# Two staging buffers instead of three for q and k, and w_in loaded by column halves, in a fused attention and gMLP kernel

## The chip, the cores and the metric

The kernel runs on one core of a Trainium2 chip. The core has a matrix engine (TensorE, PE in the profile; its weight loads are PEld), a vector engine (VectorE, DVE), a scalar engine (ScalarE, ACT), GpSimd (POOL) and a queue engine (SyncE, SP). Each runs its own instruction stream in order; they meet at semaphores. Data between main memory and the on-chip memory is moved by 16 DMA engines; here SP issues DMAs on one queue (q1 in the profile) and POOL on another (q0). The metric is the device time of one execution in microseconds.

## The reference

Two blocks follow one another. The first is attention with a window and sinks: 4 batches, 8 heads, 768 positions, head size 64; position s sees positions s-127 to s and the first 4. The second is a gated MLP over the positions.

```python
scores = 0.125 * q @ k^T ; keep = is_sink | in_window       # per batch and head
a = softmax(where(keep, scores, -1e9)) ; x = a @ v           # x: (4, 768, 512)
h = gelu_tanh(x @ w_in)                                      # w_in: (512, 1024)
u, v = h[..., :512], h[..., 512:]
v_n = (v - mean) / sqrt(var + 1e-6) * g_ln
v_s = einsum('ts,bsd->btd', w_sg, v_n) + b_sg                # w_sg: (768, 768)
out = x + (u * v_s) @ w_out                                  # w_out: (512, 512)
```

The columns of w_in are thus of two kinds: the first 512 give u, the last 512 give the v of the MLP.

## The kernel before

**Pairs.** Attention goes by pairs of heads: 16 pairs, numbered n from 0, four to a batch. For each pair the kernel loads k and q (`load_qk`, line 79, on SP's queue, 384 KB each as float32 into the pool `loads`) and v (`load_v`, line 86, on POOL's queue, cast to bf16 on the way, 128 bytes per row and head; four tiles `v_bufs` in turn). Line 179 (`repack`) casts k and q to bf16 and joins the two heads: pair 0 on VectorE, all others on POOL. Once the cast has read a staging tile, that tile is free for a later load; the pool gives tiles out in turn, so its number of buffers says how many pairs back the cast lies that a load must wait for. Line 185 transposes k and q on TensorE (`keys`, `queries`), line 192 copies the result to SBUF on ScalarE, line 202 copies the four sink columns into `sk` on POOL.

**One pass of the loop** over n does the scores of pair n (line 220), their exponentials (224) and the mask (231), the sinks' scores (235, 237), and the product with v of pair n-1 (`values`, lines 265, 268, 271). In each group of three query tiles, line 271 adds the sinks' part from `vsink`, one tile with the sink rows of v for all pairs, loaded by two small DMAs on POOL's queue (line 132) right behind the first v tile. At the start of pass n POOL casts pair n+2, issues the v load of pair n+2 and then the weights that are due (`load_weights(n)`): w_in in passes 0 to 3, w_sg in pass 4, b_sg, g_ln and w_out in pass 5. `load_qk(n+3)` stands in pass n, but SP's queue holds nothing else before the first transpose by DMA (line 281), so at the start a load is issued as soon as its buffer is free.

**The MLP** of a batch follows when its four pairs are done: `hidden` computes the v half (`hidden_v`, line 293, w_in's last 512 columns) and then the u half (`hidden_u`, line 305, the first 512); `inverse_root` and `normalise` (333) work on VectorE. The spatial product (343) and the projection (354) are put into a list of fillers that are dealt out between the attention steps of the next batch. Results go out on SP's queue (360). After the first batch, three pairs in four have their columns transposed by DMA (281), also on SP's queue. The order of all instructions on each engine is the order of the program text; nothing reorders it.

A last part (`stable_path`) runs only if a sum is out of range; it doesn't run with these inputs.

Of the kernel before, what the change touches and what calls it, by code (L numbers as in the profile page):

```python
# [17 lines left out]
def kernel(  # L18
# [14 lines left out]
    nc = tc.nc  # L33
# [5 lines left out]
    d_ff = moe_w_in.shape[1]  # L39
    DF = d_ff // 2  # L40
    NT = S // 128
    HP = H // 2
    KD = DM // 128
# [4 lines left out]
    NH = S // 2  # L48

    consts = ctx.enter_context(tc.tile_pool(name="consts", bufs=1))  # L50
    loads = ctx.enter_context(tc.tile_pool(name="loads", bufs=3))
    work = ctx.enter_context(tc.tile_pool(name="work", bufs=2))
    small = ctx.enter_context(tc.tile_pool(name="small", bufs=4))
    ps_s = ctx.enter_context(tc.tile_pool(name="ps_s", bufs=2, space=PSUM))
# [88 lines left out]
    w_in_sb = consts.tile([128, KD, d_ff], BF16, name="w_in_sb")  # L143
# [4 lines left out]
    wsgT = consts.tile([128, NT, S], BF16, name="wsgT")  # L148

    def load_weights(n):  # L150
        if n < KD:
            nc.gpsimd.dma_start(out=w_in_sb[:, n, :],
                                in_=moe_w_in[128 * n:128 * (n + 1), :])
        elif n == 4:
            for c in (slice(0, HT), slice(HT, NT)):
                nc.gpsimd.dma_start(
                    out=wsg_sb[:, c, :],
                    in_=moe_w_sg.rearrange("(c p) s -> p c s", p=128)[:, c, :])
        elif n == 5:
            nc.gpsimd.dma_start(out=b_bc, in_=moe_b_sg.partition_broadcast(128))  # L160
            nc.gpsimd.dma_start(out=g_sb, in_=moe_g_ln.rearrange("(c p) -> p c", p=128))
            nc.gpsimd.dma_start(out=w_out_sb,
                                in_=moe_w_out.rearrange("(c p) f -> p c f", p=128))
# [351 lines left out]
    for n in range(NP):  # L515
        if n + 2 < NP:
            repack(n + 2, G)
            load_v(n + 2)
        load_weights(n)
        value = (lambda i: values(n - 1, i)) if n > 0 and valued < n - 1 else (lambda i: None)  # L520
        points = (HT + 1) * ((HP - n) % HP)
# [79 lines left out]
```

## Time and profile before

| | |
|---|---|
| median of 3 runs | 192.22 us (190.65 to 193.03) |
| the profiled execution | 192.91 us |
| its span, first to last instruction | 191.2 us |
| TensorE busy | 159.4 us, 83% |
| VectorE busy | 152.4 us, 80% |
| ScalarE busy | 115.9 us, 61% |
| GpSimd busy | 57.2 us, 30% |
| q1 (SP): q, k, transposes, results | 20.65 MB, 35.9% of the DMA engines' time |
| q0 (POOL): v, sinks, weights | 6.31 MB, 35.3% |

Busy time is the time in which an engine executes; waiting and issuing aren't in it. The DMA shares are means over the whole span; the first 48 us are far above them (nine tenths or more in the page's slices from 5 to 48 us). The megabytes count what is written, so v and the weights, which become bf16, have half of what is read.

### The profile page before, as it was taken

The numbers are of one execution on the slowest core, as the hardware profiler recorded it, in microseconds if no ns is written. First come the engines' busy times: TensorE is split into PE (matmuls) and PEld (weight loads), VectorE is DVE, ScalarE is ACT, GpSimd is POOL, SyncE is SP. The second block draws the span as 40 slices with busy tenths as digits, with TensorE's granted clock in tenths as the row PEclk, the third lists the DMA queues.
The fourth block names the chain that finished last, engine by engine and source line by source line (L and its number), as shares of the span: only waits on it lengthen the run. The fifth ranks groups of instructions, "written<-read, shape, count | busy, mean of one in ns | idle before, by whom it ended". The sixth has DMA issues, their size and how long they took to land.

```text
span 191.2 us, 3722 instructions
## 1 busy us (share of the span) xinstructions
PE 159.4 (83%) x1407; PEld 88.7 (46%) x1407; DVE 152.4 (80%) x362; ACT 115.9 (61%) x159; POOL 57.2 (30%) x98
## 2 busy tenths in 40 slices
PE   0661977879969999989979999899799979998960
PEld 0321655535553655545535555355355444545420
DVE  5780578879974999869889999698999976989960
ACT  2381699976871766866796686966966533740000
POOL 7497567970024016145006024163000000000000
PEclk9999999999975999999999999999999999999997
DMA  5999999999276075999653869996202172000072
GB/s 183 287 304 261 254 235 210 156 197 189 47 206 41 3 206 62 256 301 167 46 125 89 81 216 183 322 225 43 41 3 41 55 211 111 0 0 3 0 279 66
DMA packets 46777, 27.27 MB, mean 143 GB/s; under 512 B 33632, under 2 KB 43104, under 8 KB 46752
## 3 DMA queue, kind: packets, MB, share of 16 engines
q1 hardware_dynamic: 19360, 20.65, 35.9%
q0 software_dynamic: 27392, 6.31, 35.3%
q8 instruction: 13, 0.21, 0.5%
q14 instruction: 12, 0.10, 0.2%
HBM read 24.81 MB, written 6.29 MB: 163 GB/s over the span
## 4 chain that ended last, share of the span: by engine, by line
PE 44%; DVE 30%; ACT 11%; DMA 8%; issue 4%; POOL 0%; DVEq 0%
PE vs L343 11%; PE o_ps L354 10%; DMA vsink<-in_v_dram 8%; ACT ex L224 6%; DVE st L297 5%; PE sc L220 5%; DVE ex L231 4%; PE hv L293 4%; PE cps L185 4%; DVE vn L333 3%; DVE gv L346 3%; PE hu L305 3%; PE av L265 3%; DVE o_sb L357 2%; ACT kT L192 2%
## 5 line engine op out<-in xcount | busy, mean ns | idle before, releaser
L224 ACT ACTIVATE ex<-sc 128x1024 bf16<-128x1024 f32 (+1 forms) x48 | 45.6, 958 | 19.4 <-PE sc L220 19.1
L343 PE MATMUL vs<-wsgT,vn 128*128 128x384 bf16 x192 | 38.3, 339 | 2.6 <-DVE vn L333 1.0
L231 DVE TENSOR_TENSOR ex<-ex,mask 128x1024 bf16<-128x1024 bf16 x32 | 24.4, 764 | 3.1 <-ACT ex L224 3.1
L343 PEld LDWEIGHTS <-vn 128*128 128x128 bf16 x192 | 18.3, 101 | 16.9 <-issue 4.3
L354 PE MATMUL o_ps<-w_out_sb,gT 128*128 128x512 bf16 x96 | 24.1, 379 | 0.8 <-DVE o_sb L357 0.8
L293 PE MATMUL hv<-w_in_sb,xT 128*128 128x512 bf16 x96 | 22.8, 379 | 2.2 <-DVE xT L246 1.8
L305 PE MATMUL hu<-xT,w_in_sb 128*128 128x384 bf16 x128 | 23.6, 325 | 0.0
L179 POOL CAST k_bf<-k_sb 128x768 bf16<-128x768 f32 x15 | 12.8, 850 | 36.0 <-DMA k_sb<-in_k_dram 29.9
L265 PE MATMUL av<-v_sb,ex 128*128 128x65 bf16 x192 | 19.0, 198 | 5.1 <-DMA v_sb<-in_v_dram 3.2
L346 DVE SCALAR_TENSOR_TENSOR gv<-vs,g_sb,b_bc 128x384 bf16<-128x384 f32 x32 | 19.6, 612 | 3.0 <-PE vs L343 3.0
L295 ACT ACTIVATE v_all<-hv 128x512 f32<-128x512 f32 x24 | 14.3, 597 | 11.9 <-PE hv L293 11.8
L202 POOL COPY sk<-kT 64x4 bf16<-64x4 bf16 x32 | 7.0, 218 | 46.9 <-ACT kT L192 45.9
L265 PEld LDWEIGHTS <-ex 128*128 128x128 bf16 x192 | 14.9, 100 | 13.0 <-issue 5.7
L220 PE MATMUL sc<-qT,kT 64*128 64x256 bf16 x192 | 19.3, 285 | 1.2 <-DVE qT L194 1.1
L297 DVE BATCH_NORM_STATS2 st<-v_all 128x6 f32<-128x512 f32 x24 | 16.4, 683 | 4.8 <-ACT v_all L295 4.6
L308 ACT ACTIVATE uT<-hu 128x384 bf16<-128x384 f32 x32 | 15.7, 490 | 7.1 <-PE hu L305 6.9
L276 DVE TENSOR_TENSOR x<-av,inverses 128x384 bf16<-128x384 f32 x32 | 17.8, 557 | 1.1
L192 ACT COPY kT<-cps 128x768 bf16<-128x768 bf16 x16 | 12.7, 794 | 9.3 <-PE cps L185 9.3
L357 DVE TENSOR_TENSOR o_sb<-o_ps,x 128x512 f32<-128x512 f32 x24 | 16.5, 687 | 2.0 <-PE o_ps L354 1.7
L268 PE MATMUL av<-v_sb,ex 128*128 128x65 bf16 x160 | 17.4, 197 | 0.0
L86 POOL DMA_DIRECT2D v_sb<-in_v_dram x16 | 16.5, 1032 | 0.0
L305 PEld LDWEIGHTS <-w_in_sb 128*128 128x128 bf16 x128 | 12.1, 97 | 8.3 <-issue 1.2
(72 smaller groups left out, 232.5 us busy)
## 6 DMA issues: line engine op xcount, KB each, us to landing
k_sb<-in_k_dram SPq DMA_DIRECT2D x16, 384.0 KB, 6.0
q_sb<-in_q_dram SPq DMA_DIRECT2D x16, 384.0 KB, 6.5
out_dram<-o_sb SPq DMA_DIRECT2D x24, 256.0 KB, 3.7
v_sb<-in_v_dram POOLq DMA_DIRECT2D x16, 192.0 KB, 6.7
wsg_sb<-in_moe_w_sg_dram POOLq DMA_DIRECT2D x2, 576.0 KB, 9.6
w_in_sb<-in_moe_w_in_dram POOLq DMA_DIRECT2D x4, 256.0 KB, 11.7
w_out_sb<-in_moe_w_out_dram POOLq DMA_DIRECT2D x1, 512.0 KB, 10.3
b_bc<-in_moe_b_sg_dram POOLq DMA_DIRECT2D x1, 384.0 KB, 8.9
```

Source lines behind the costliest of these rows:

```text
L220: nc.tensor.matmul(sc[:, hl, w:w + n_q], kT[rows, 128 * j:128 * (j + 1)], qT[rows, 128 * j:128 * j + n_q], start=True, stop=True)
L224: nc.scalar.activation(out=part, in_=sc[:, :, 0:w], func=AF.Exp, scale=scale)
L231: nc.vector.tensor_mul(part, part, m)
L265: nc.tensor.matmul(av[:, m, hl, :], probs(i, hl, 0), v_sb[:, hl, i, :], start=(m == 0 and hl == 0), stop=False)
L276: nc.vector.tensor_mul(x_sb[b][:, hp, HT * c:HT * (c + 1), :].rearrange("p i (h d) -> p i h d", h=2), av[:, :, :, 0:64], rcp.to_broadcast( ...
L293: nc.tensor.matmul(h_ps, xT[b][:, c, 128 * j:128 * (j + 1)], w_in_sb[:, c, DF:], start=(c == 0), stop=(c == KD - 1))
L297: nc.vector.bn_stats(out=st, in_=v_alls[b][:, j, :])
L305: nc.tensor.matmul(h_ps[:, 0:NH], w_in_sb[:, c, 128 * f:128 * (f + 1)], xT[b][:, c, NH * n:NH * (n + 1)], start=(c == 0), stop=(c == KD - 1))
L343: nc.tensor.matmul(vs[:, 0:NH], vns[b][:, si, 128 * f:128 * (f + 1)], wsgT[:, si, cols], start=(si == 0), stop=(si == NT - 1))
L346: nc.vector.scalar_tensor_tensor(out=gv, in0=vs[:, 0:NH], scalar=g_sb[:, f:f + 1], in1=b_bc[:, cols], op0=ALU.mult, op1=ALU.add)
L354: nc.tensor.matmul(o_ps, gTs[b][:, c, 128 * t:128 * (t + 1)], w_out_sb[:, c, :], start=(c == 0), stop=(c == KU - 1))
L357: nc.vector.tensor_add(o_sb.rearrange("p (h d) -> p h d", h=HP), o_ps.rearrange("p (h d) -> p h d", h=HP), x_sb[b][:, :, t, :])
```

## The change

The pool `loads` gets two buffers per name instead of three, so k and q of pair n+2 wait for the cast of pair n (before: pair n+3 for pair n). w_in, which was loaded in four DMAs of one block of 128 rows and all 1024 columns, is loaded in four DMAs of two blocks of rows and 512 columns, the last 512 columns (the MLP's v half) in passes 0 and 1 and the first 512 (u) in passes 2 and 3. The bytes are the same.

```diff
-    loads = ctx.enter_context(tc.tile_pool(name="loads", bufs=3))
+    loads = ctx.enter_context(tc.tile_pool(name="loads", bufs=2))
...
     def load_weights(n):
-        if n < KD:
-            nc.gpsimd.dma_start(out=w_in_sb[:, n, :],
-                                in_=moe_w_in[128 * n:128 * (n + 1), :])
+        if n < 4:
+            half = slice(DF, d_ff) if n < 2 else slice(0, DF)
+            cs = slice(KD // 2 * (n % 2), KD // 2 * (n % 2 + 1))
+            nc.gpsimd.dma_start(
+                out=w_in_sb[:, cs, half],
+                in_=moe_w_in.rearrange("(c p) f -> p c f", p=128)[:, cs, half])
```

## The prediction

> **What bounds the kernel now.** I read the chain that ended last first, for where the time to the end is spent, then the engine timelines around the piece that stands out, then the DMA traffic there. The chain in order of time has one piece that is no computing (start us, us, what):
>
> ```profile
> 3.65 0.63 POOL vsink L132
> 4.29 15.00 DMA vsink<-in_v_dram
> 19.29 0.14 issue
> 19.42 0.27 PE av L271
> 19.69 1.28 PE cps L185 x12
> ```
>
> Fifteen of 191.2 us go to the arrival of the sink rows, 8 KB. TensorE's timeline shows what that costs (in brackets the idle time before, and who ended it):
>
> ```profile
> 13.22 0.61 PE L220 MATMUL sc<-qT,kT 64*128 64x256 bf16 x4
> 17.04 0.32 PE L265 MATMUL av<-v_sb,ex 128*128 128x65 bf16 x3 [3.21 <-DMA v_sb<-in_v_dram]
> ...
> 19.42 0.27 PE L271 MATMUL av<-vsink,exs 128*128 128x130 bf16 x1 [1.68 <-DMA vsink<-in_v_dram]
> ...
> 24.70 0.27 PE L265 MATMUL av<-v_sb,ex 128*128 128x65 bf16 x3
> ```
>
> TensorE stands 3.21 us for the first v tile and 1.68 us for the sinks, 4.89 us together; VectorE waits 5.81 us at the same place for the result. After it TensorE is near its limit (stage, length, then busy us and count of PE, PEld, DVE, ACT, POOL, clock, DMA share, GB/s):
>
> ```profile
> 70.00:95.00 25.00, 24.42 (x217) 13.35 (x214) 21.83 (x56) 17.74 (x27) 9.17 (x13) 1.00 0.89 181
> 95.00:135.00 40.00, 38.07 (x352) 20.62 (x348) 35.78 (x84) 30.61 (x42) 12.72 (x20) 1.00 0.75 154
> ```
>
> 62.5 us busy of 65: whatever the start gains or loses arrives at the end nearly whole.
>
> Why are 192 KB of v so late? They were issued at 2.19 us and landed 14.8 us later, on POOL's queue (q0), beside the q and k loads on SP's queue (q1). Packets from 8 to 12 us, then from 19.5 to 20.5 us:
>
> ```profile
> q1 hardware_dynamic: 772, 1.11, 90.1%
> q0 software_dynamic: 773, 0.10, 37.4%
> ...
> q0 software_dynamic: 1139, 0.15, 227.0%
> q1 hardware_dynamic: 19, 0.02, 7.9%
> ```
>
> While both queues have work they take turns packet by packet: 193 per us each, a 1536-byte piece of q or k against a 128-byte piece of v. When q1 is dry, q0 does 1139 per us. A v load without q1 traffic (issued at 33.32 us) took 4.9 us instead of 14.8.
>
> **Part 1: two buffers.** Every engine keeps its instruction order; only the wait of a load changes, from the cast three tiles back to the cast two back. SP's queue before:
>
> ```profile
> 2.84 0.47 SPq L79 DMA_DIRECT2D k_sb<-in_k_dram  x1
> ...
> 4.68 0.37 SPq L79 DMA_DIRECT2D k_sb<-in_k_dram  x1
> ...
> 8.61 0.37 SPq L79 DMA_DIRECT2D k_sb<-in_k_dram  x1
> ...
> 15.79 0.37 SPq L79 DMA_DIRECT2D k_sb<-in_k_dram  x1
> ```
>
> These are pairs 2, 3, 4 and 6; the releases behind them stay (VectorE's cast of k 0 ends at 4.66, POOL's of k 1 at 8.58). So the releases now let out one pair earlier in number: pair 2 at 4.68 (q at 5.65), pair 3 at 8.61 (9.85), pair 4 at 11.69 or a little later.
>
> In steps. (a) Pairs 0 and 1 are four loads of 272 packets (256 data, 16 for completion). From the start to 7.0 us q1 moved 1009 packets, so pair 1 is through at about 7.4 us, as before. (b) Pair 2 follows in its old place or up to 1.5 us later: two loads of 272/193 = 1.4 us, 2.8 us. (c) Pair 3 is issued at 8.61, where pair 4 is now. How soon do its packets move? The fence shows: k of pair 6 was issued at 15.79, yet q1 moved only 19 packets from 19.5 to 20.5. From issue to packets are some 3.8 us or more while q0 is busy. So pair 3 moves from about 12.4 us, where pair 4 begins now. (d) Between 7.4 and 12.4 us q1 has 2.8 us of work instead of 5: a hole of about 2.2 us (2.8 if pair 4 is today a little behind its queue). (e) Up to 9.75 us q0 had moved 475 packets; the first v tile (1536 + 16) and the sinks (2 x 80) need 1712. The other 1237, less 193 per us of sharing, fit into the hole at 1139 per us. v and sinks leave the queue by 12.5 us; a landing follows the last packet by 1 to 2 us: by about 13.8.
>
> TensorE is ready for v at 13.83, VectorE's last mask multiply ends at 13.92. So both waits go: the ceiling is 4.89 us.
>
> **What is late next: the second v tile.** It landed at 23.2 and is first read at 24.70; with the start 4.9 earlier it is wanted at 19.8. It was issued at 9.76, and from 12.4 us on q1's traffic is as before (pair 3 in the place of pair 4, and so on). By 12.6 us q0 had moved 1089 of the 1712 packets ahead of it; the other 623 cost 623/193 = 3.2 us, which it no longer waits. But its own packets may not be ready then: the first tile's, issued at 2.19, came after 6 us (21 of them by 7.0), four us later; that makes 13.8 here and leaves 2.0 us. So it lands between 20.0 and 21.2. I take 20.9, near the end that has a row of its own: TensorE stands 1.1 us, and **3.8 us** stay of 4.89. The third v tile (landed 25.0, wanted at 29.23 - 3.8 = 25.4) and the fourth (30.5 against 30.0, itself some 2 us earlier) then pass.
>
> **Cost of the shorter prefetch.** Nothing but later loads stands behind a waiting load on SP before 51.5 us. From then on the release lies far back: load 9 is issued at 67.66, its new release (cast of k 7) ended at 37.3; load 11 at 82.91 against 72.3; load 15, the closest, q at 122.52 against 115.3. The transposes and the stores in SP's queue set those issues, so the edit costs nothing there. At the start POOL may wait for a load ahead of a cast; queued behind are the next v load, w_in and the sink copies. If pairs 2 and 3 take the 8.5 and 8.9 us that the loads issued at 4.68 and 5.65 take now, k 2 is cast at 13.2 instead of 10.83 and q 2 at 14.6 instead of 11.89; TensorE wants them at 14.6 and 15.2. Bounds: 0 to 0.3 us; I take 0, as TensorE's transposes now follow the casts of pairs 3 to 5 by 6 to 9 us.
>
> **Part 2: w_in.** Four loads in the same places, each half the rows' width over two row blocks: 1024 packets of 1 KB instead of 512 of 2 KB. Nearest rows: w_out in 1 KB pieces ran at 0.21 MB per us (47 to 48 us), w_sg in 1.5 KB pieces at 0.19 (37.5 to 38.5), so the bytes cost the same within a tenth: -0.5 to 0.5 us of q0 over all four. POOL's issue was 0.56 us for one row per partition and 0.78 for four (w_out): 0 to 0.9 us more in all, where POOL idles 70%. What it buys: the v half is complete with the second load (landed 31.7) instead of the fourth (36.7). Line 293 waits for xT, not for w_in (1.25 us before 39.48); 3.8 us earlier it would want the fourth block at 35.7, which is then also about 2 us earlier. So the edit is worth 0, at most 1 us where the old order would have been late. The u half, last to land at 36.7, is read at 44.39 - 3.8 = 40.6.
>
> **Skill against trace.** The Trainium skill, "DMA: Bandwidth & Descriptors", section "Queues, rings and completion order", says that an engine round-robins between queues but drains a whole packet, typically 9 to 17 descriptors, before it switches. If v's pieces went nine at a turn, the first tile would hardly suffer from q1, and thinning q1 would bring about 0 instead of 3.8. The rows above, 772 against 773, show pieces of 128 bytes taking one turn each; the measurement decides.
>
> **Sum.** 192.91 (profiled run; span 191.2 and 1.7 around it) - 3.8 = 189.1. The median of the runs is 192.22, 0.7 below that run; from it 188.4, which I forecast.
>
> **Rivals.** (1) The second v tile is no limit: q1 has a further gap near 16 to 17 us, since pair 5 waits for a later cast. All 4.89 go: 187.3. For it: v needs few turns in a gap. Against: its landing lagged by 3 us now. 0.27. (2) The change doesn't do what it says: pair 3 starts 1.2 us after its issue, as the very first load does (landed 3.2 us after issue), the queue never runs dry, v lands as now: 191.7 to 192.2. Against it stands step (c). 0.19, with small holes. (3) Slower: with two buffers each pair's landing time L is paid in series. Pair 5 would land at 8.61 + L + 0.9 + L, and TensorE wants it at 34.17 - 3.8 = 30.4. It costs from L = 10.4 on and eats the whole gain from L = 12.3; at 14, q0's latency now, pair 5 lands 37.5 and is 7.1 us late: 192.2 - 3.8 + 7.1 = 195.5. For it: L is 7.2 to 8.9 already. Against: those values come from a longer queue. 0.08. The forecast itself, 187.5 to 189.4, has 0.46.
>
> **Numbers.** Two per cent, about what a measurement of this kernel can tell, lies at 188.4. Faster by more: 0.27 and nearly half of 0.46, 0.47. Slower by more: 0.06. Within: 0.47. The range leaves out the slower case and the lower tail: 186.8 to 192.3. Not in it by design: TensorE ran at half clock from 56 to 62 us in this run (5.5 us busy); if that spell moves, up to 2.8 us go either way.
>
> **What would show it.** Right: SP issues k of pair 2 at 4.7 and of pair 3 at 8.6; q1 nearly empty for two us between 9 and 12.5; the sinks' chain piece ends near 13.8; a wait of about 1 us on the second v tile; no wait of line 293 on w_in. Wrong: pair 3 moving by 10 us, the sinks still landing past 17, or POOL's casts waiting so long that TensorE's transposes wait for POOL.

## The result and the profile after

The changed kernel takes 186.59 us (median of four runs, 184.96 to 186.89) against 191.85 us before: a ratio of 0.9705, 95% interval 0.963 to 0.978. It is 5.3 us faster; the forecast was 3.8 us (188.4), and its range, 186.8 to 192.3, began 0.2 us above the measured median. The profiled execution took 184.96 us with a span of 183.1 us. It is the quickest of its four runs, while the profiled execution before was one of the slower ones, so the two profiles differ by 8 us. Some executions of every version are a per cent or two slower than the others, mostly at a lower granted clock; the medians below include them, the ratios leave them out.

The chain that ended last no longer has the sinks in it. In order of time (start us, us, what) the longest pieces of its start, after the issues on SP, are:

```profile
2.33 6.00 DMA q_sb<-in_q_dram
...
8.38 0.97 POOL q_bf L182
...
9.40 0.83 PE cps L188 x6
...
10.25 0.80 ACT qT L195
```

What was fifteen microseconds of waiting for 8 KB is now the arrival of q of pair 1. The lines are three higher than before (185 is now 188, 265 is 268, 271 is 274, 293 is 296). TensorE's timeline at the two old waits:

```profile
12.73 0.61 PE L223 MATMUL sc<-qT,kT 64*128 64x256 bf16 x4
13.28 0.34 PE L268 MATMUL av<-v_sb,ex 128*128 128x65 bf16 x3
...
13.82 0.30 PE L274 MATMUL av<-vsink,exs 128*128 128x130 bf16 x1
...
18.70 0.27 PE L268 MATMUL av<-v_sb,ex 128*128 128x65 bf16 x3
```

No line has a bracket: TensorE waits neither for the first v tile, nor for the sinks, nor (last line) for the second v tile. That last row stood at 24.70, so 6.0 us are gained by here: 0.49 because pair 1's loads land 0.6 us earlier (the scores of 12.73 stood at 13.22), 4.89 for the two waits, 0.4 at the end of pass 1, where TensorE's clock is up sooner (from the sinks' scores to the second v tile 1.30 us instead of 1.72; the full clock is granted from 17.35 us, before from 24.69), and 0.2 in small pieces around the old waits.

The queues show how. Packets of q1 (q and k) and q0 (v, sinks, weights) in three windows, 7 to 8, 10 to 12 and 13.5 to 15 us:

```profile
q0 software_dynamic: 1034, 0.13, 201.4%
q1 hardware_dynamic: 45, 0.06, 18.1%
...
q1 hardware_dynamic: 496, 0.72, 104.5%
q0 software_dynamic: 6, 0.00, 0.2%
...
q0 software_dynamic: 1247, 0.16, 165.2%
q1 hardware_dynamic: 116, 0.17, 37.2%
```

Before, from 8 to 12 us, both queues had work all the time and shared the slots evenly, 193 packets per us each. Now they alternate: for most of the time one queue runs alone while the other's next load is on its way. The first v tile landed at 10.3 us (17.0 before), the sinks at 10.9 (19.3), the second v tile at 16.2 (23.2). SP issued k of pair 2 when the prediction said (4.68), k of pair 3 0.7 us before the predicted 8.61, and k of pair 4 0.8 us after 11.69:

```profile
4.70 0.37 SPq L79 DMA_DIRECT2D k_sb<-in_k_dram  x1
...
7.87 0.37 SPq L79 DMA_DIRECT2D k_sb<-in_k_dram  x1
...
12.53 0.37 SPq L79 DMA_DIRECT2D k_sb<-in_k_dram  x1
```

### The profile page after: what moved, and what is told of

It is laid out like the page before. It is cut to its first block, busy times and chain, and to the rows that moved or that the text cites. A ratio compares the mean times of both kernels' runs of the same rounds, so it can differ in the third digit from the quotient of the medians.

```text
span 183.1 us, 3710 instructions
## 1 busy us (share of the span) xinstructions
PE 156.4 (85%) x1397; PEld 88.4 (48%) x1407; DVE 150.6 (82%) x362; ACT 115.7 (63%) x159; POOL 58.3 (32%) x98
## 4 chain that ended last, share of the span: by engine, by line
PE 58%; DVE 17%; ACT 13%; issue 4%; DMA 3%; SPq 1%; POOL 1%; DVEq 0%
PE vs L346 13%; PE o_ps L357 11%; ACT ex L227 6%; PE sc L223 6%; PE hv L296 6%; PE hu L308 6%; PE cps L188 5%; DVE st L300 4%; PE av L268 4%; DMA q_sb<-in_q_dram 3%; ACT kT L195 2%; DVE vn L336 2%; PE av L271 2%; PE wps L171 2%; PE av L274 2%
## 5 line engine op out<-in xcount | busy, mean ns | idle before, releaser
L346 PE MATMUL vs<-wsgT,vn 128*128 128x384 bf16 x192 | 36.4, 326 | 3.3 <-DVE vn L336 1.4
L346 PEld LDWEIGHTS <-vn 128*128 128x128 bf16 x192 | 17.8, 98 | 16.6 <-DVE vn L336 4.0
L234 DVE TENSOR_TENSOR ex<-ex,mask 128x1024 bf16<-128x1024 bf16 x32 | 22.7, 709 | 3.6 <-ACT ex L227 3.6
L357 PE MATMUL o_ps<-w_out_sb,gT 128*128 128x512 bf16 x89 | 23.4, 379 | 0.9 <-DVE o_sb L360 0.6
L298 ACT ACTIVATE v_all<-hv 128x512 f32<-128x512 f32 x24 | 14.3, 597 | 11.8 <-PE hv L296 11.5
L205 POOL COPY sk<-kT 64x4 bf16<-64x4 bf16 x32 | 6.6, 206 | 34.4 <-ACT kT L195 33.5
L182 POOL CAST q_bf<-q_sb 128x768 bf16<-128x768 f32 x15 | 14.6, 972 | 5.0 <-PE hu L308 2.1
```

Source lines behind the costliest of these rows:

```text
L182: eng.tensor_copy(flat.rearrange("p t (h d) -> p h t d", h=2), src)
L234: nc.vector.tensor_mul(part, part, m)
L346: nc.tensor.matmul(vs[:, 0:NH], vns[b][:, si, 128 * f:128 * (f + 1)], wsgT[:, si, cols], start=(si == 0), stop=(si == NT - 1))
L357: nc.tensor.matmul(o_ps, gTs[b][:, c, 128 * t:128 * (t + 1)], w_out_sb[:, c, :], start=(c == 0), stop=(c == KU - 1))
```

## The experiments

Times of before differ a little between chips (190.2 to 191.9); each ratio is to before on the same chip. The changed kernel was run three times: 186.59 (0.9705), 186.23 and 185.91 (0.972, interval 0.967 to 0.977). By these two ratios it gains 5.3 to 5.7 us.

### Two buffers alone

```diff
-    loads = ctx.enter_context(tc.tile_pool(name="loads", bufs=3))
+    loads = ctx.enter_context(tc.tile_pool(name="loads", bufs=2))
```

> Two buffers, w_in loaded as before (four blocks of 128 rows, all columns). If the whole gain comes from the gaps that two buffers leave in SP's queue at the start: 5 to 6 us faster than before (186 to 187), and the line that computes the v half waits for xT, or for the fourth block of w_in by less than 0.5 us. If w_in's new order carries part of it: the fourth block lands at 34 to 36 us, is wanted at about 32, and 1 to 3 us of the gain are missing (187.5 to 190).

Measured: 189.44 us (187.59 to 193.46), ratio 0.9926 (0.9874 to 0.9978). By the ratio 1.4 us are left of the gain; the changed kernel on the same chip took 186.23. The start is quick (the first exponentials of pass 4 begin at 29.25 us; 30.12 in the changed kernel's profile on the same chip, 33.87 in the profile before), but then TensorE stands at the products with w_in (line 293):

```profile
33.46 0.38 PE L293 MATMUL hv<-w_in_sb,xT 128*128 128x512 bf16 x1 [0.38 <-DMA w_in_sb<-in_moe_w_in_dram]
37.03 0.59 PE L293 MATMUL hv<-w_in_sb,xT 128*128 128x512 bf16 x1 [3.20 <-DMA w_in_sb<-in_moe_w_in_dram]
```

The fourth block, issued at 28.23, landed at 37.0 us, and TensorE idled 3.2 us. About one of them it idles in the changed kernel too, for xT: from those exponentials to the first gelu it is 8.4 us here and 5.8 there, so 2.6 us are net. Then TensorE's clock is at half for 3.4 us (the product at 37.03 takes 0.59 us instead of 0.38), and at the fifth gelu the distance is 13.5 us against 9.4. The medians differ by 3.2 us, and by the ratios some 4 us of the gain are missing: a little more than the 1 to 3 us that were expected.

### w_in alone

```diff
-        if n < KD:
-            nc.gpsimd.dma_start(out=w_in_sb[:, n, :], ...
+        if n < 4:
+            half = slice(DF, d_ff) if n < 2 else slice(0, DF)
...
```

with three buffers.

> w_in by column halves, three buffers as before. If the buffers make the difference: as before within 0.5 us (191.4 to 192.4), with the sinks landing at 19 us again. If the order of w_in matters by itself: 1 us or more away from before.

Measured: 190.38 us, ratio 1.0018 (0.9985 to 1.0052). No effect by itself. The old waits are there (2.20 us for v, 2.02 for the sinks in its profile). By the ratios w_in alone brings nothing, two buffers alone 1.4 us, both together 5.3 to 5.7: the order of w_in removes the wait that two buffers uncover.

### Only pair 2 held back, with each order of w_in

```diff
+    def buffer(n):
+        return (0, 1, 0)[n] if n < 3 else (2, 1, 0)[n % 3]
...
-            dst = loads.tile([128, 2, NT, 64], F32, name=name)
+        for src, dst in zip((k, q), kq_bufs[buffer(n)]):
```

Three buffers, but pair 2 takes the buffer of pair 0.

> Three buffers and w_in as before, but pair 2 uses the buffers of pair 0, so that its loads wait for pair 0's cast (4.7 us) and all later loads wait, as before, for the cast three pairs back. If the one gap near 7 to 8.3 us is what lets the first v tile and the sinks through: the sinks land before 13 us, both waits (4.9 us) go, and the time falls by 4 to 6 us (186 to 188). If the queue must stay thin throughout for the second and third v tiles: the waits move to the second v tile, which lands at 19 us or later, and only 1 to 4 us are gained (188 to 191).

> Pair 2 held to pair 0's cast, three buffers otherwise, and w_in by column halves. In the run with pair 2 held and the old w_in the second v tile landed at 21.3 us and cost 1.9 us of waiting. If a thin queue is needed throughout, that wait stays and this kernel is 1 to 3 us slower than the changed one (187.5 to 189.5 where the changed one has 186.2). If the first gap is all that the buffers give, it equals the changed kernel within 0.7 us.

Measured: 188.9 us with the old order of w_in, ratio 0.9921 (0.9871 to 0.9971), and 188.46 with the new one, 0.9893 (0.9799 to 0.9987). One gap is enough for the first v tile and the sinks (landed at 11.0 and by 12 in the first of the two). But once pair 2 is out, the next loads follow at once and both queues share again; the second v tile lands at 21.3 and 21.6 us, and the wait has moved there (1.90 us, here, and 1.63):

```profile
21.35 0.25 PE L268 MATMUL av<-v_sb,ex 128*128 128x65 bf16 x3 [1.90 <-DMA v_sb<-in_v_dram]
```

So the queue has to stay thin after the first gap: the interval of the second kernel lies above both intervals of the changed kernel. Here the prediction's limit, the second v tile, is real; with two buffers it isn't.

### The gap where the prediction drew it

```diff
+    def buffer(n):
+        return n if n < 2 else (2, 1)[n % 2]
```

Pair 2 is loaded at once, as before; from pair 3 on two buffers turn. w_in by halves.

> w_in by column halves. Pairs 0, 1 and 2 have a buffer each, so pair 2 is loaded at once as before; from pair 3 on only two buffers turn, so each load waits for the cast two pairs back. SP's queue then has its first gap only after pair 2, from about 9.8 us, as the prediction drew it. If the prediction's place of the gap were enough: the first v tile and the sinks land by 13.8 us and the time equals the changed kernel's within 1 us (186 to 187.5). If the earlier gap of the changed kernel (7 to 8.3 us) is what matters: the first v tile lands after 13.8 and 1 to 3 us are missing (187.5 to 189.5).

Measured: 185.55 us, ratio 0.973 (0.964 to 0.982), as the changed kernel within the intervals. q1 was thin from 10 to 11.5 us (116 packets; at 193 per us it would be 290), the first v tile landed at 14.2 us and the sinks at 14.7, a little after the 13.8 of the expectation; TensorE came to v at 14.97 and to the sinks at 15.52 and waited for neither (pair 1 was late here too). Whether the first gap comes at 7 or at 10 us made no difference that this run can tell, because TensorE came late enough; where it comes sooner, as with the late transposes below, the later gap costs a wait. That there is a gap, and that the queue stays thin, is what counts.

### One buffer

```diff
-    loads = ctx.enter_context(tc.tile_pool(name="loads", bufs=2))
+    loads = ctx.enter_context(tc.tile_pool(name="loads", bufs=1))
```

> The changed kernel with a single buffer for q and for k: each load waits for the cast of the pair before it. The forecast's slower case with its strongest cause: landing time and cast in series for every pair. With a landing time of 4 to 5 us and 1.7 us of casts a pair takes 6 us or more where the loop needs 4.5, so five pairs of the start lose 5 to 10 us against the changed kernel: 190 to 196. If the loop has slack enough to hide it: within 2 us of the changed kernel.

Measured: 190.31 us, ratio 0.9969 (0.9922 to 1.0015): as before, and 4 us or more behind the changed kernel. The first v tile lands at 7.1 us, earlier than anywhere, and q and k land 3.1 to 6.2 us after issue. But landing and cast now follow one another. From the list of waits, first 40 us (engine, line, releaser: us in total, times, longest):

```profile
POOL k_bf L182 <- DMA k_sb<-in_k_dram: 5.6, 3, 2.5
POOL q_bf L182 <- DMA q_sb<-in_q_dram: 4.1, 4, 1.9
...
PE cps L188 <- POOL k_bf L182: 2.7, 2, 1.8
...
PE cps L188 <- POOL q_bf L182: 1.5, 2, 0.8
PE scs L238 <- POOL sk L205: 1.3, 1, 1.3
```

TensorE waits 5.5 us for POOL in the last three rows. This is the mechanism of the prediction's slower case, reached with one buffer; it eats the gain, but no more. With two it doesn't arise: q and k took 4.6 to 7.4 us from the third pair on in the changed kernel's profile, under the 10.4 us from which it would have cost.

### The changed kernel again, and pair 1's transposes later

> The changed kernel again, on the same chip as the three others: 186.6 within 0.7 us. TensorE's full clock begins near 17.4 us, and a spell of half clock follows 30.7 us later; if that spell's length (one or two stretches of 3.4 us) is a matter of chance, it differs from the first profile in some of these runs; if it follows from the earlier start, it is one stretch again.

Measured: 186.23 us (183.7 to 186.82), 4.1 us under before on that chip by the medians. TensorE's full clock began at 18.8 us by the trace's clock records, not near 17.4, and there was no spell of half clock at all until the end (see the last section). This profile starts 2 us later than the first one:

```profile
9.68 0.82 PE L188 MATMUL cps<-iden,k_bf 128*128 128x128 bf16 x6 [1.21 <-POOL k_bf L182]
11.97 0.82 PE L188 MATMUL cps<-iden,q_bf 128*128 128x128 bf16 x6 [1.47 <-POOL q_bf L182]
```

q of pair 1 landed at 10.4 us (8.3 in the first profile), and two of pair 0's score groups stand behind its transposes. So in this profile the start hangs on the arrival of pair 1. The next kernel moves the transposes:

```diff
-            if g == 0 and n + 1 < NP:
+            if g == (HT - 1 if n == 0 else 0) and n + 1 < NP:
                 keys(n + 1)
```

> The changed kernel, but in pass 0 the transposes of pair 1 come after all three score groups of pair 0 instead of after the first. In the changed kernel TensorE waits at 8.2 to 12 us for the casts of pair 1 (0.4 us in one profile, 2.7 in another), with two score groups of pair 0 queued behind. If the arrival of pair 1 is what bounds the changed kernel's first 13 us: 0.5 to 2 us faster than the changed kernel and less spread between runs. If ScalarE bounds it (its five pieces take 5.1 us there in any order): the same within 0.5 us.

Measured: 184.47 us (183.68 to 185.44), ratio 0.968 (0.960 to 0.976). Its profile has pair 1 landing as late as in the second profile of the changed kernel (8.8 and 10.1 us), and yet TensorE begins pass 1 at 12.79 us with waits of 0.17 and 0.34 us. It has the lowest median of the study. Against the changed kernel, which ran on other chips, the ratio is lower by 0.003 to 0.004 (0.5 to 0.8 us) and the intervals overlap, so a gain over it is not shown; the trace shows only that the late arrival no longer holds up the start.

### Both variants together, and products to warm TensorE

The three-then-two buffers with the late transposes; then the same with 38 products of the identity before the first work:

```diff
+            nc.tensor.matmul(warm[:, 0:128], iden, iden, start=True, stop=True)
...
+    warm_up(30)
     keys(0)
     queries(0, V, ps_m, "mm")
+    warm_up(8)
```

> The two variants that were at least as fast as the changed kernel, together: a buffer each for pairs 0 to 2 and two in turn from there, w_in by halves, and pair 1's transposes at the end of pass 0. With the late transposes alone 184.5 was measured, with the three-then-two buffers alone 185.6, with the changed kernel 186.2. If their gains add: 183.5 to 184.2. If both only cover the same late arrival of pair 1: 184.3 to 185.5. In the first case pass 1 starts with no wait for pair 2; in the second the sinks, which land at 14.6 us with three-then-two, are waited for by about 1 us.

> As the kernel before it in this list, plus 38 matrix products of the identity with itself at the start, 30 before the first transpose and 8 before the first scores; nothing reads their result. TensorE's transposes take 0.82 us per six in the first 17 us and 0.50 later. If the early speed is a matter of TensorE having stood idle, the six take 0.5 us by 8 us and 0.5 to 1.5 us are gained. If it doesn't matter, because ScalarE and the loads set the pace up to 14 us: the same within 0.4 us.

> The changed kernel beside the two variants, on their chip: 186 to 186.8; this is what the variants' times are compared with.

Measured on one chip: 184.91 (0.9674, 0.9624 to 0.9723), 185.26 (0.9685, 0.9628 to 0.9742) and, for the changed kernel, 185.91 (0.972, 0.967 to 0.9771). The intervals overlap, and no added gain shows. In the profile of the first one TensorE, with the transposes out of the way, comes to the first v tile too early (1.58 us of waiting at 14.84). The warm-up raises the clock early and saves no time that these runs can tell; its clock is told in the last section.

### Whole blocks of w_in, two per pass

```diff
-        if n < KD:
-            nc.gpsimd.dma_start(out=w_in_sb[:, n, :], ...
+        if n < KD // 2:
+            for c in (2 * n, 2 * n + 1):
+                nc.gpsimd.dma_start(out=w_in_sb[:, c, :], ...
...
```

Two buffers; all of w_in in passes 0 and 1.

> Two buffers, w_in in its old blocks of 128 rows and all columns, but two blocks in pass 0 and two in pass 1, so that the last block is issued where the second v half is issued in the changed kernel, with twice the bytes ahead of it. With one block per pass the wait for w_in was 3.6 us and the time 189.4. If that wait is the whole difference to the changed kernel: no wait for w_in, 185.5 to 187. If the form of the pieces matters (1 KB instead of 2 KB) or the doubled bytes early in the queue delay the v tiles: 187.5 to 189.5, with waits for v tiles before 30 us.

Measured: 187.77 us, ratio 0.9834 (0.9761 to 0.9907). The wait for w_in is gone (the last block landed at 32.8 us, and TensorE came to it only at 34.34, after a wait for xT), but v tiles come late: one issued at 24.00, behind all of w_in, landed at 36.29.

```profile
29.14 0.25 PE L268 MATMUL av<-v_sb,ex 128*128 128x65 bf16 x3 [1.01 <-DMA v_sb<-in_v_dram]
...
36.34 0.24 PE L268 MATMUL av<-v_sb,ex 128*128 128x65 bf16 x2 [1.61 <-DMA v_sb<-in_v_dram]
```

So loading all of w_in early removes one wait and makes others; loading early only the half that is wanted early removes it without a new one. The times say this less sharply than the traces: the interval here overlaps the changed kernel's, and the size of the pieces (2 KB here, 1 KB there) differs too and was not tested by itself.

## Why the prediction was right and where it was wrong

**What bounds the start: right.** Both waits, 4.89 us, were due to q0 sharing the slots with q1, and both went when q1 was held back, also where only pair 2 was.

**Steps (a) to (e): right in kind, but the gap came sooner.** Pair 2 was issued at 4.70 as said, pair 3 at 7.87 instead of 8.61. But the delay from issue to packets held for pair 2 as well, about 3.4 us, so the gap came before pair 2 and not behind it: q1 was nearly empty from 7 to 8 us, v and the sinks had left the queue by 9 instead of 12.5, and they landed some 2 us later, not 1 to 2. The run with the gap near its predicted place (10 to 11.5 us) reached the same time.

**What is late next: wrong. This is the step that failed.** I took 1.1 us of waiting for the second v tile, on the ground that from 12.4 us on q1's traffic is as before. It isn't: with two buffers the loads find a shorter queue, their latency falls (k of pair 4 took 4.7 us, where loads of that time took 7.5), and new gaps open again and again (q1 moved 4 packets from 17.5 to 19 us). The second v tile landed at 16.2 us, not 20.9, and was waited for by nobody. The runs with pair 2 alone held back show that my picture, one gap and then the old traffic, gives just such a wait: the tile lands at 21.3 us and costs 1.9 us.

**Part 2 at 0 to 1 us: wrong too.** Without the new order of w_in the kernel is 3.2 us slower by the medians, some 4 us by the ratios. I let the fourth block land 2 us earlier than 36.7 because the queue would be ahead; but POOL issues it only after the casts of its pass, at 28.23 instead of 29.62, and it took 8.8 us instead of 7.1. It landed at 37.0, while the product that wants it would have had its xT at about 34.4 (1.9 us after the first product of the group, as in the changed kernel; the first is at 32.49). I had set 34.7 against 35.7. Both sides of that comparison were off: the block later than I thought, the work earlier. It didn't hurt the forecast, which took no wait there; it hurts the account of where the gain lies.

**Missing terms.** Pair 1 landed 0.6 us earlier, worth 0.5 us in that profile; that is luck, for in the second profile its q landed as late as 10.4 (8.3 in the first; 10.1 with three buffers on the second's chip). TensorE's clock came up 7 us sooner, worth 0.4, and 0.2 lie in small pieces. Together with the 1.1 us that weren't lost, 3.8 becomes 6.0 at 18.7 us, which the profile shows. The ratios keep 5.3 to 5.7 us of it; the varying arrival of pair 1 (2 us between two profiles) could account for the rest, but what each run lost to it was not measured. The base moved too: the forecast started from 192.22, and before, with one more execution, has 191.85.

**The rivals.** The first, all waits gone because of further gaps, is what happened, but the gap that let the second v tile through came at 13.5 to 15 us, not at 16 to 17, and the time fell below its 187.3. The second (no gap) is refuted by the packet counts. The third shows with one buffer only, and there at 190.31, not 195.5.

**One piece per turn.** The prediction read turns of one piece each from 772 packets against 773. That was too little: nine pieces of each per turn would give equal counts as well. The packet starts in the trace before decide it. From 9 to 10 us, pieces of either queue start again and again 86 ns after one another, and 16 engines that move one piece of each queue per 86 ns give 186 per us, near the 193 counted. So the turn here is one piece, against the nine or more descriptors that the section cited in the prediction gives.

## What to carry to other kernels

Prefetch that goes deeper than its consumer needs is not free when another queue feeds the same engines: here the third buffer kept one queue full at the start, and each small piece on the other waited for a large one. Look for the transfer that is needed next and count what shares its slots; then, when a stall goes, look at every later transfer with its issue time and its new deadline, because a load that was just in time is the next stall. An edit that is worth nothing alone can be worth 3 to 4 us beside another one.

## What the runs showed of the hardware

The first load of any run, with nothing else moving, landed 3.0 to 3.3 us after its issue. Later loads began to move later. If SP's packets are counted off in the order of issue, 272 to a load, k of pairs 2 to 7 in the changed kernel began 1.6 to 3.8 us after its issue (pair 2 at about 8.1 us, pair 4 at 14.2, pair 7 at 28.6), while POOL's queue had work. With one buffer k of pairs 2 and 3, issued at 10.36 and 15.20, began after 1.0 us. What sets the delay is open.

TensorE's granted clock went up and down in visible steps. In the run with the warm-up products, six transposes take 0.52 us at 4.61 and 0.85 us again at 14.19; the granted clock in three windows (stage, length, PE, PEld, DVE, ACT, POOL busy, clock, DMA share, GB/s):

```profile
4.64:11.47 6.83, 3.56 (x47) 2.45 (x45) 5.18 (x19) 4.12 (x6) 3.94 (x7) 1.00 1.25 271
11.47:18.30 6.83, 5.32 (x53) 3.72 (x54) 3.37 (x7) 5.11 (x8) 6.00 (x9) 0.50 1.48 262
18.30:25.00 6.70, 5.64 (x95) 4.05 (x94) 6.14 (x14) 6.64 (x10) 5.58 (x11) 1.00 1.50 261
```

It came up at 4.64 us, 3.2 us after the products began, and fell again at 11.47, after a stretch with TensorE busy for 3.56 of 6.83 us. So warming an engine that then has to wait gained nothing here. The Trainium skill, "TensorE: Matmul & The Clock Gate", section "Part 1: The HAM clock gate (the "warmup" mystery)", gives about 3.4 us of sustained activity for the full clock; the 3.2 us here are near it. The half-clock spells before the end of the kernel lasted 3.41 or 6.83 us. The spell after the first batch's MLP is not set by the kernel alone: of these two profiles of the changed kernel one is at half clock for part of 45 to 50 us and the other isn't.

```profile
45.00:50.00 5.00, 3.14 (x35) 2.23 (x33) 4.13 (x9) 4.14 (x6) 0.37 (x2) 0.81 1.04 171
```

```profile
45.00:50.00 5.00, 3.16 (x37) 1.98 (x36) 4.11 (x10) 4.57 (x7) 0.18 (x1) 1.00 0.79 144
```

TensorE's busy time is about the same in the two rows, but the second profile runs some 2 us behind the first, so they don't hold quite the same work. What decides about the spell is open: in the 3.41 us just before the first profile's clock fell, at 48.07, TensorE was busy for 1.55 us. In the profile before, the spell lasted 6.83 us, and from the first exponentials of pass 4 to those of pass 7 that profile takes 1.9 us more than the first one after. That is a part of the 8 us between the two profiles that no run ties to the edit.
